# An attention and expert-routing kernel: a new order of work inside each pair of heads

## The chip, the cores and the metric

The kernel runs on one core of one Trainium2 chip. The metric is the device time of one execution in microseconds. In what follows PE is the matmul engine (TensorE), PEld its weight loads, DVE is VectorE, ACT is ScalarE, POOL is GpSimd and SP is SyncE, which only issues transfers here.

## The reference

The first half is attention with chunk selection for 4 batches, 8 heads, 768 positions and 64 channels. The second half sends every token to its best one of 8 experts.

```python
k_min, k_max = k_chunks.min(axis=3), k_chunks.max(axis=3)      # 24 chunks of 32 keys
ub = sum(maximum(q * k_min, q * k_max), over channels)          # a bound per query and chunk
top_chunks = the 6 chunks of largest ub, among those up to the query's own
scores = q @ k.T / 8, only in those chunks and only for keys up to the query
attn = softmax(scores);  x = attn @ v                           # heads side by side: (3072, 512)

logits = x @ w_gate;  expert = argmax(logits);  gate = softmax(logits)[expert]
out[token] = gate * (relu(x[token] @ w1[expert]) @ w2[expert])
```

## The kernel before

**Pairs.** The work is cut into 16 pairs of heads. Pair `i` is heads 2`hp` and 2`hp`+1 of batch `b`, with `b, hp = divmod(i, 4)`. Keys and queries lie transposed, channels on partitions: `KTE` and `QSB`, two buffers each, the pairs taking turns. The causal scores of a pair come in seven units `u`, each 128 keys by at most 384 queries for two heads (list `units`, L286). Units 0 and 1 belong to the first half of the queries (`qb` 0), units 2 to 6 to the second (`qb` 1).

**Steps of one pair.** Every step is a small function, and each belongs to one engine.

- `k_mm`, `q_mm` (PE, L192 and L219) transpose the loaded keys and queries into PSUM, half by half. `k_a` and `q_a` (ACT, L203, L228, L231) and `k_v`, `q_v` (DVE, L197, L198, L223) evict them. A cast on POOL (L229), put into the list `late`, fills the other half of `QSB`. `kse` (DVE) makes the chunk sums and differences.
- `ub` (PE, L238) computes the bounds, `ub_a` (ACT, L245) evicts them, `sel_mm` (PE, L250) transposes them. `sel_v` (DVE, L256 to L267) adds the causal bias, takes the eight largest of each row and marks the chunks that are not selected in `nsel`. `mask` (PE, L274) transposes the marks and `mask_a` (ACT, L280) copies them into rows of `QSB`, where they act as a penalty inside the score matmul.
- `scores` (PE, L298), `exps` (ACT, L314, then on POOL for blocks on the diagonal a triangle select, L318), `av` (PE, L331: probabilities times values, two heads on two halves of the array), `add` (DVE, L339: adds the unit's probabilities to those of the first unit, for the row sums). `o_ev(i, qb)` evicts the output of one half, on DVE (L346) or ACT (L344).
- `ud` (PE, L362 and L374, four 32-column tiles) computes row sums and unnormalized router logits, `ud_a` (ACT, L380) evicts them, `lgp_mm` (PE, L385) transposes them to `pl`. `lgp_v` (DVE, L391 and L395) takes the reciprocal and writes the scaled logits to `lgt`; a closure `sums` (POOL, L403 or L406), put into the list `sums_`, adds `lgt` to the batch's logits `lg`. `x_mm` (PE, L415) transposes the output to `px`, and `x_v` (DVE, L420) normalizes it into the token rows `xrow`.
- In pairs with `hp` 1 of batches 1 to 3 (`router`) the router of the batch before runs as well: `logits`, `expo`, `rank_mm`, `rank_v`, `gates`. `scatter` (POOL, L493) then writes the token rows to memory by expert.

**Order.** The order on every engine is written out by hand: `tc.manual_schedule` keeps each engine's instructions in program order. The main loop (L810) has four groups `g` for each pair `i`, and mixes steps of pair `i` with those of the pairs before and after: the output and router steps of pair `i`-1, the selection of pair `n` = `i`+1, the keys and queries of pair `m` = `i`+2. `flush(late)` and `flush(sums_)` emit the collected POOL steps at the place where they are called; `pieces` issues the next expert weight loads on POOL (L157). `first_pair` (L683) does pair 0 and the beginning of pair 1.

**Buffers.** The PSUM pool `ps_m` has three buffers; `pk`, `pq`, `pu`, `pt`, `pm`, `pl` and `px` take turns in them, in program order. `ps_s` has two buffers for scores and `ps_o` one for the output. In SBUF the probabilities have four buffers (`Pr`), and `lgt` has one.

**After the pairs.** `table` (DVE) works out which expert each tile of 128 tokens belongs to and where its rows are (`grow`). `gather` (POOL, L593) fetches the rows, `x_in` (SP, L605) transposes them, `up` (PE, L641) and `down` (PE, L653) are the expert's two matmuls, and the results are scattered to the output (POOL, L661).

The softmax here doesn't subtract the row's maximum and nothing guards it: scores larger than these inputs give would overflow.

## Time and profile before

| | us |
|---|---|
| median of 3 runs | 358.19 (357.07 to 358.97) |
| the profiled execution | 357.17 |
| its span, first to last instruction | 355.5 |
| PE busy in the span | 329.2 |
| ACT, DVE, POOL busy | 230.4, 229.5, 186.7 |
| first `ub` of pair 1 (end of most of the first pair) | 20.99 |
| first scores of unit 2 of pair 15 | 223.75 |
| first expert matmul | 236.43 |

The profile is one execution. A row of its timeline gives the start, the duration, the engine, the line, the operation, what is written and read, the number of instructions joined in the row, and in brackets how long the engine had been idle and what ended that. The duration of a row with several instructions runs from the start of the first to the end of the last. [...] the step from one start to the next says how much of PE's time an instruction takes. A busy share is a mean over the span, which here has two stages: the pairs of heads, in which all engines work, and the experts, in which DVE has little to do.

### The profile page before, as it was taken

To read this page: it belongs to the slowest core of one execution; us is meant where nothing else is said; L and a number is where in the kernel's file an instruction comes from. 1 tells how busy PE (TensorE), PEld (TensorE's weight loads), DVE (VectorE), ACT (ScalarE), POOL (GpSimd) and SP (SyncE) were. 2 spreads that over 40 slices of the span, in tenths; PEclk is the share of its full clock that TensorE was granted. 3 is DMA by queue.
4 is the path that set the end of the run, shared out by engine and by line. 5 is a ranking of instruction groups with operands and counts; after the bars stand their busy time and mean duration, and the time that the engine had idled before them with its cause. 6 is when DMAs were issued, how large, how long until landed. Compare 5 with 4: busy or idle time off the path is not lost. (4 is left out here: it accounts for less than half of the span.)

```text
span 355.5 us, 7585 instructions
## 1 busy us (share of the span) xinstructions
PE 329.2 (93%) x2382; PEld 177.2 (50%) x2392; DVE 229.5 (65%) x776; ACT 230.4 (65%) x373; POOL 186.7 (53%) x300
## 2 busy tenths in 40 slices
PE   7889999999999999999999999977995899999992
PEld 7545656556555555555565555534441344444440
DVE  6688999999999999999999999941730000000000
ACT  2588788788796887886887977613323454544551
POOL 8515434536475437284355477583574556655323
PEclk9999999999999999999999999989998999999999
DMA  9998998899585897765979954969694999998962
GB/s 175 205 209 152 167 184 169 153 190 167 104 211 113 161 178 155 152 171 114 186 137 181 182 122 113 209 124 197 137 227 121 227 185 216 194 231 160 216 154 80
DMA packets 132071, 59.83 MB, mean 168 GB/s; under 512 B 122811, under 2 KB 122813, under 8 KB 132032
## 3 DMA queue, kind: packets, MB, share of 16 engines
q1 hardware_dynamic: 120640, 29.91, 43.5%
q0 software_dynamic: 11392, 29.42, 40.0%
q8 instruction: 21, 0.34, 0.4%
q14 instruction: 18, 0.15, 0.1%
HBM read 56.14 MB, written 10.51 MB: 188 GB/s over the span
## 5 line engine op out<-in xcount | busy, mean ns | idle before, releaser
L339 DVE TENSOR_TENSOR Pa<-Pa,Pr 128x768 f32<-128x768 f32 (+2 forms) x109 | 80.5, 742 | 4.3
L318 POOL TENSOR_SCALAR_AFFINE_SELECT Pr<-Pr 128x256 f32<-128x256 f32 x78 | 36.9, 492 | 77.9 <-ACT Pr L314 77.9
L314 ACT ACTIVATE Pr<-ps 128x768 f32<-128x768 f32 x79 | 62.6, 819 | 10.7 <-ACT KTE L203 4.3
L653 PE MATMUL py<-w_all,hT 128*128 x220 | 52.4, 379 | 3.0 <-issue 1.7
L298 PE MATMUL ps<-QSB,KTE 128*128 128x384 bf16 (+4 forms) x352 | 50.4, 283 | 1.5 <-ACT Pr L314 0.2
L661 POOL DMA_INDIRECT out_dram<-y,ti_all x28 | 28.0, 1001 | 37.2 <-ACT y L660 32.1
L298 PEld LDWEIGHTS <-KTE 128*128 128x128 bf16 (+1 forms) x352 | 26.5, 102 | 28.4 <-issue 22.0
L641 PE MATMUL ph<-w_all,KTE 128*128 x116 | 31.1, 413 | 6.3 <-ACT h__3986 L644 3.6
L653 PEld LDWEIGHTS <-hT 128*128 128x128 bf16 x224 | 21.8, 98 | 29.5 <-issue 1.8
L314 ACT ACTIVATE Pa<-ps 128x768 f32<-128x768 f32 x32 | 26.0, 812 | 14.0 <-PE ps L298 12.6
L660 ACT ACTIVATE y<-py,gt_all 128x512 f32<-128x512 f32 x27 | 18.6, 687 | 25.0 <-PE py L653 19.4
L203 ACT ACTIVATE KTE<-pk 64x384 bf16<-64x384 f32 x60 | 29.3, 488 | 7.1 <-DVE kmn L198 6.7
L493 POOL DMA_INDIRECT xs_dram<-xrow,sli x24 | 25.6, 1065 | 7.8 <-issue 5.7
L641 PE MATMUL ph<-w_all,QSB 128*128 x94 | 22.6, 379 | 1.6 <-DMA QSB<-xgqT 1.5
L641 PEld LDWEIGHTS <-KTE 128*128 128x128 bf16 x120 | 12.3, 104 | 23.0 <-issue 9.6
L280 ACT ACTIVATE QSB<-pm 24x640 bf16<-24x640 bf16 x30 | 20.8, 692 | 2.8 <-PE pm L274 2.1
L614 DVE TENSOR_TENSOR ti_all<-xgqA,inv_i 128x1 int32<-128x1 int32 x9 | 1.4, 160 | 30.7 <-DMA xgqA<-xs_dram,grow 26.1
L157 POOL DMA_DIRECT2D w_all<-in_moe_w_dram x32 | 21.1, 663 | 0.0
L197 DVE TENSOR_REDUCE kmx<-pk 128x12 f32<-128x384 f32 x32 | 17.6, 549 | 3.2 <-PE pk L192 3.0
L593 POOL DMA_INDIRECT xgqT<-xs_dram,grow x14 | 14.8, 1058 | 9.1 <-issue 6.2
L593 POOL DMA_INDIRECT xgqA<-xs_dram,grow x14 | 14.4, 1029 | 8.6 <-issue 4.7
L614 DVE TENSOR_TENSOR ti_all<-xgqT,inv_i 128x1 int32<-128x1 int32 x8 | 1.3, 159 | 25.7 <-DMA xgqT<-xs_dram,grow 20.9
(318 smaller groups left out, 635.9 us busy)
## 6 DMA issues: line engine op xcount, KB each, us to landing
w_all<-in_moe_w_dram POOLq DMA_DIRECT2D x32, 512.0 KB
out_dram<-y,ti_all POOLq DMA_INDIRECT x28
t__115<-in_k_dram SPq DMA_DIRECT2D x2, 192.0 KB
t__118<-in_q_dram SPq DMA_DIRECT2D x2, 192.0 KB
t__121<-in_v_dram SPq DMA_DIRECT2D x2, 192.0 KB
t__218<-in_k_dram SPq DMA_DIRECT2D x2, 192.0 KB
t__240<-in_q_dram SPq DMA_DIRECT2D x2, 192.0 KB
t__243<-in_v_dram SPq DMA_DIRECT2D x2, 192.0 KB
```

The costliest lines, as they stand in the source:

```text
L157: nc.gpsimd.dma_start(out=dst, in_=src.rearrange("(c p) f -> p c f" if n < 2 else "(p c) f -> p c f", p=128))
L203: nc.scalar.activation(kte[0:64, hd, ts(hf, 384)], pt[64 * hd:64 * hd + 64, :], AF.Copy, bias=0.0, scale=0.125)
L280: nc.scalar.activation(qsb[64:64 + NCH, hd, 128:S], s["pm"][32 * hd:32 * hd + NCH, 128:S], AF.Copy)
L298: nc.tensor.matmul(ps[ds(h * n, n), hd, ds(c0, w)], lhsT=kte[:, hd, ds(kb * 128 + h * n, n)], rhs=qsb[:, hd, ds(qb * 384 + 384 - w, w)], s ...
L314: nc.scalar.activation(P[:], ps[:, :, 0:384], AF.Exp)
L318: nc.gpsimd.affine_select(out=pd, in_=pd, pattern=[[0, 2], [1, 128]], compare_op=ALU.is_ge, fill=0.0, base=0, channel_multiplier=-1)
L339: nc.vector.tensor_tensor(acc[:, :, 384 - w:384], acc[:, :, 384 - w:384], P[:, :, ds(c0, w)], ALU.add)
L493: d = nc.gpsimd.indirect_dma_start(out=xs_dram[:], out_offset=bass.IndirectOffsetOnAxis(ap=sli[:, u:u + 1], axis=0), in_=bst[b][f"xrow{u % ...
L593: d = nc.gpsimd.indirect_dma_start(out=xg_bufs[j % XB].bitcast(I32), out_offset=None, in_=xs_dram[:], in_offset=bass.IndirectOffsetOnAxis( ...
L641: nc.tensor.matmul(ph[:, fh, :], lhsT=xT[:, c, :], rhs=w_all[:, ds(wo + (c * F + fh * 512), 512)], start=(c == 0), stop=(c == NDC - 1), sk ...
L653: nc.tensor.matmul(py[:], lhsT=hT[:, c, :], rhs=w_all[:, ds(wo + (W1W + c * DM), DM)], start=(c == 0), stop=(c == NFC - 1))
L661: d = nc.gpsimd.indirect_dma_start(out=out[:], out_offset=bass.IndirectOffsetOnAxis(ap=fs[j]["ti"], axis=0), in_=y[:], in_offset=None, bou ...
```

## The change

The loop over four groups is written out as one sequence with a new order. Output 0 is evicted on ACT in all pairs. `ub` of pair `m` stands at the end of iteration `i`, behind `av` 4, 5 and 6; before, the same `ub` stood in the next iteration, behind `av` 0 and 1. `sel_mm` and `sel_v` follow scores 2 and 3, `mask` follows `k_mm(0)`, `ud` comes ahead of `av` 2 and 3, and `mask_a` comes ahead of exp 6 on ACT. `lgp_mm` and `x_mm(0)` follow scores 6. `q_a` copies the absolute values of both halves first and then the two halves of the queries. The chunk adds of units 1 and 4, 5 and 6 move to other places on DVE. The first pair computes the bounds with positions on partitions at once (`pt0`), without eviction and transposition, for five blocks of 128 positions, two and then three at a time.

```diff
@@ consts_first: the first pair's own bias and marks
-        nc.gpsimd.memset(cbias[:], 0.0)
...
+        cb0 = work.tile([128, NQ, NCH], FP32, tag="xrow", bufs=3, name="cb0")
...
+        ns0 = work.tile([128, NQ, 2, 32], BF16, tag="xrow", bufs=3, name="ns0")
...
+    def consts_bias():
+        nc.gpsimd.memset(cbias[:], 0.0)
...
@@ first_pair
         consts_last()
-        consts_route(colf)
-        prep[0]["ub"]()
-        prep[0]["ub_a"]()
+        pt = ps_m.tile([128, NQ, 2, NCH], FP32, tag="m", name="pt0")
+        for j in range(NQ):
+            for w_, nm in ((0, "qT"), (1, "qA")):
+                nc.tensor.matmul(pt[:, j], lhsT=s[nm][:].rearrange("p a c -> p (a c)")[:, ds(128 * j + 128, 128)],
+                                 rhs=KSD[0][:, w_, :, 0:NCH], start=(nm == "qT"), stop=(nm == "qA"),
+                                 skip_group_check=True)
         kt(1)
-        spin(8)
-        prep[0]["sel_mm"]()
-        spin(20)
+        spin(28)
...
         for _ in range(2):
             load_w(next(wnext))
+        consts_bias()
...
-        select(0)
-        mask_mm(0)
-        mask_in(0)
+        halves = (range(0, 2), range(2, NQ))
+        select(halves[0])
+        consts_route(colf)
+        mask_mm(halves[0])
+        mask_in(halves[0])
...
@@ the main loop, iteration i, as it is now
+            if i > 0:
+                if i < NP - 1 and not (hp == 2 and b > 0):
+                    pieces(i, 2 if router else 1)
+                if router:
+                    logits()
+                for u in (2, 3):
+                    scores(i, u)
+                    exps(i, u)
+                run(rout, i - 2, "x_mm", 1)
+                run(prep, n, "sel_mm")
+                add(i - 1, 6)
+
+                xv_first = hp != 2 or b == 0
+                if xv_first:
+                    run(rout, i - 2, "x_v", 1)
+                run(prep, n, "sel_v")
+                if not xv_first:
+                    run(rout, i - 2, "x_v", 1)
+
+                av(i, 0)
+                av(i, 1)
+                o_ev(i, 0, True)
...
+            for u in (4, 5):
+                scores(i, u)
+                if u == 5:
...
+                        if router:
+                            rank_mm()
+                            expo()
+                            rank_v()
+                            gates()
+                        run(prep, m, "k_mm", 0)
+                        run(prep, m, "k_a", 0)
+                        run(prep, n, "mask")
+                exps(i, u)
+
+            run(rout, i - 1, "ud")
+            run(rout, i - 1, "ud_a")
+            if i > 0:
+                add(i, 1)
+                run(prep, n, "mask_a")
+                run(prep, m, "k_v", 0)
+            av(i, 2)
+            av(i, 3)
+            add(i, 3)
+            flush(late)
+            if i < NP - 1:
+                pieces(i, 4)
+            scores(i, 6, True)
+            exps(i, 6)
...
+            if not router:
+                add(i, 4)
+            if i == NP - 2:
+                next(early_table)
...
+            run(rout, i - 1, "lgp_mm")
+            run(rout, i - 1, "x_mm", 0)
...
+            flush(sums_)
...
+            run(rout, i - 1, "lgp_v")
+            run(rout, i - 1, "x_v", 0)
+            run(prep, m, "k_mm", 1)
+            run(prep, m, "k_a", 1)
+            if n < NP:
+                for u in (0, 1):
+                    scores(n, u)
+                    exps(n, u)
+            run(prep, m, "k_v", 1)
+            for hf in range(2):
+                run(prep, m, "q_mm", hf)
+                run(prep, m, "q_v", hf)
+                run(prep, m, "q_a", hf, 0)
+            for hf in range(2):
+                run(prep, m, "q_a", hf, 1)
...
+            run(prep, m, "kse")
+
+            av(i, 4)
+            av(i, 5)
+            av(i, 6)
+            if router:
+                add(i, 4)
+            if i < NP - 1:
+                add(i, 5)
+            o_ev(i, 1, i >= NP - 2)
+            run(prep, m, "ub")
+            run(prep, m, "ub_a")
+            if hp == 0 and b > 0:
+                flush(sums_)
```

The removed lines of the loop, which held the same steps in the four groups, stand in the listing above.

## The prediction, written before the changed kernel had run

> **What bounds the kernel now.** I read the busy table first, then windows cut from one `ub` to the next (one pair of heads each), then the timeline of such a window, then the waits. "us" from the span's start.

> ```profile
> PE 329.2 (93%) x2382; PEld 177.2 (50%) x2392; DVE 229.5 (65%) x776; ACT 230.4 (65%) x373; POOL 186.7 (53%) x300
> ```
> ```profile
> 60.90:74.41 13.51, 13.44 (x116) 7.66 (x114) 12.62 (x38) 11.20 (x20) 6.42 (x12) 1.00 0.88 167
> 87.91:102.29 14.38, 14.08 (x129) 8.05 (x127) 13.83 (x50) 11.71 (x22) 7.55 (x13) 1.00 0.67 140
> 102.29:116.60 14.31, 13.57 (x116) 7.64 (x114) 13.61 (x39) 11.32 (x20) 7.20 (x13) 1.00 0.72 154
> ```
> The windows' columns are length, then busy PE, PEld, DVE, ACT, POOL. A plain pair takes 13.51 us with PE busy throughout, and DVE, 12.62 us, has only 0.9 us to spare. In the router pair (second row) and the one behind it DVE is the fuller engine. So PE sets the pace, and any wait on DVE reaches it at once. The end of a plain pair shows how near it comes:

> ```profile
> 65.14 0.50 PE L298 MATMUL ps<-QSB,KTE 128*64 128x256 bf16 x8
> 65.72 0.81 ACT L314 ACTIVATE Pr<-ps 128x768 f32<-128x768 f32 x1 [0.54 <-ACT KTE L203]
> 66.61 1.48 POOL L318 TENSOR_SCALAR_AFFINE_SELECT Pr<-Pr 128x256 f32<-128x256 f32 x2 [0.38 <-ACT Pr L314]
> 66.88 2.02 DVE L339 TENSOR_TENSOR Pa<-Pa,Pr 128x768 f32<-128x768 f32 x2
> 68.06 1.55 POOL L406 TENSOR_TENSOR lg<-lg,lgt 128x96 f32<-128x96 f32 x2
> ...
> 69.64 0.42 DVE L395 TENSOR_TENSOR lgt<-pl,rec 128x96 f32<-128x96 f32 x2 [0.41 <-POOL lg L406]
> 69.98 0.55 DVE L420 TENSOR_TENSOR xrow<-px,rec 128x384 bf16<-128x384 f32 x1
> ...
> 70.17 0.97 PE L219 MATMUL pq<-ident_f,t__966 128*128 128x128 f32 x6
> ```
> This is one chain: scores of unit 6, their exponential, two triangle selects on POOL, POOL's two sums (`sums`, which read the one `lgt` buffer), then DVE may overwrite `lgt`, which frees `pl`, whose PSUM buffer `q_mm(0)` needs (three buffers; `pl`, `px`, `pk`, then `pq`); `x_v(0)` frees `px` for `q_mm(1)`. Today PE has 70.17-65.14 = 5.03 us of other work between the ends of that chain, and the chain just fits:

> ```profile
> DVE lgt L395 <- POOL lg L406: 2.4, 6, 0.4
> ```
> Total, number, longest: six waits of 0.4 us in the stage from 33 to 223 us; covered, nothing more.

> [...] The rows above stand in program order, and a 0.41 us wait of `lgt` delays `xrow` behind it. [...] 102.83 to 103.47 from the last four `ub` matmuls to full-array scores is 0.64 us for 0.54 us of streaming, about 0.10 us a change. [...] a POOL sum takes 0.39 us alone and up to 1.09 us beside the chunk adds L339.

> **The change, part by part.**

> *Tiling modes: nothing.* In PE's order before and after I count three full-array groups, three two-tile groups and the excursion to four tiles for `ud`: eight changes a pair both times. 0.

> *Output 0 to ScalarE.* DVE loses one 0.55 us copy (L346) in pairs that are no router pairs; there it was on ScalarE already. ACT gains 0.50 us (row L344). With DVE at 12.1 it is no bound in a plain pair. But `ot` now waits on ACT for `av(0)`, `av(1)`, and exp 4, `k_a(0)`, exp 5, `ud_a`, `mask_a` and exp 6 queue behind it.

> *The new order of a plain pair,* with each step's length from start to start in today's trace. Zero is the start of `av(i-1,4)`. PE: av 4,5,6 1.99, `ub` 1.18, scores 2,3 0.72, `x_mm(1)` 0.39, `sel_mm` 0.43, av 0,1 1.45, scores 4,5 0.72, `k_mm(0)` 0.42, mask 0.38 (starts 7.30), `ud` 1.11, av 2,3 1.34, scores 6 0.43 (starts 10.13), `lgp_mm` 0.39, `x_mm(0)` 0.33, `k_mm(1)` 0.33, scores 0,1 0.66, `q_mm` 0.78 (starts 12.27): 13.05 us if nothing waits, 0.46 under today's. What goes is today's wait of scores 5 for exp 3 (0.24) and of `q_mm(1)` for `x_v` (0.15). The mask's selection fits barely: `sel_v` 4.95 to 7.06 (2.11 long), mask at 7.30.

> *The wait it adds.* Between scores 6 and `q_mm(0)` only `lgp_mm`, `x_mm`, `k_mm`, scores 0,1 are left: 2.14 us of PE cover where there were 5.03. On ACT, `ot` runs at 6.28 (last av row + 0.87), exp 4, two `k_a`, exp 5 take 0.70, 1.0, 0.70 and exp 5 starts at 8.45; `ud_a` 9.15, the two mask copies 9.52 to 10.92, exp 6 to 11.73. POOL: two selects of 0.39 from 11.81, two sums of 0.39 to 13.45. DVE: `lgt` 13.5 to 13.9, `x_v(0)` to 14.39. PE: `q_mm(0)` 13.95, `q_mm(1)` 14.43, pair over at **14.92**. Even with exp 6 at the first possible moment (scores 6 + 0.58) it is 14.65.
> POOL may be later still: the select of unit 5 can start at 9.34, in the middle of DVE's `add` 3 and 4 (about 9.1 to 11.1). If each of its reads waits for one add (0.9), the casts (0.94) and one weight issue (0.57) end at 12.8, not 11.2, and the pair takes 15.9. I take the middle, 15.4.

> *Sum over the pairs.* Six plain iterations (3, 4, 7, 8, 11, 12): 15.4-13.5 = +1.9 each, +11.4. Iteration 2 has one sum (L403, 0.40) in place of two: +1.6. Iterations 6 and 10 likewise, 15.1 against 14.3 and 14.5: +1.4. Router iterations 5, 9, 13 have no sums ahead of `lgt`; DVE's order there (logits 1.45, selection, ranks and gates 1.8 us ahead of `k_v(0)`, which frees `pk` for `pl`) gives 14.9 against 14.38: +1.5. Iteration 1 has no sums: -0.5. Together **+15.4**.

> *First pair.* `pt0` takes ten matmuls in place of `ub`, its 0.44 us eviction and three transposes. No row has this form; 0.109 us (an f32 transpose) to 0.140 (its weight load) each gives 1.1 to 1.4. With 28 spins of 0.055 the first mask transposes come at 12.45 in place of 13.45; `consts_route` (1.1 us DVE) moves behind the first selection, and `cbias` (three selects and a memset, 0.9 us POOL) behind the weight issues where POOL idled 3.8 us. **-1.0** (0 to -1.5).

> *End of the pairs.* PE waited 2.03 us for gathered rows at 236.43; the gather at 227.28 waited for DVE's `grow`, 3.5 us after scores 2 of pair 15 (223.75). In the new order `grow` ends about 1.0 after them, so the gather's 9.15 us fit PE's own work: **-2.0**, bounded by that wait (0 to -2.0). Iteration 14 has no `q_mm`: -0.2. Loads on SP keep their order and move with the pairs; w_all issues on POOL too (counted above); nothing waits for them.

> Sum: 15.4-1.0-2.0-0.2 = **+12.2**. The profiled execution took 357.17 us, 355.5 of it span: 369.4. The median of the runs, 358.19, stands 1.0 above it, so I forecast **370.4 us**.

> **Rivals.**
> [...] Every POOL read meets an add: 15.9 in all plain pairs, +2.4 times six, iterations 2, 6, 10 another 0.6 each, routers unchanged: +20.2, less 3.2: 375. For it: L318 rows of 1.48 us for two. Against: at 11.8 DVE stands still, waiting for that very sum. 0.17.
> *Lighter.* exp 6 early and POOL free: 14.65, +1.15 times six, the other terms halved (+1.75): +8.6, less 3.2: 364. 0.14.
> *Faster.* The sums are done before DVE comes to `lgt`; then a plain pair takes 13.1 and the DVE-bound ones 0.6 less: -0.4 times eight, -0.6 times five, less 3.2: -9.4, 349. It decides if POOL's sums end before 11.7, that is 1.75 us sooner than worked out. For it: DVE loses 0.55 us, two PE waits vanish. Against: scores 6 are issued at 10.13. 0.08.
> *Nothing.* The wait shrinks to about 0.4 a pair and the first pair and the end pay for it, or the grouping does no more than keep eight mode changes: 358. 0.04.

> **How the numbers follow.** The main case has 0.57, and 370.4 is its time. Three cases are slower, 0.88; one within 0.5% (some 1.8 us, about what a measurement here tells from no change), 0.04; one faster, 0.08. The range, 360.0 to 377.0, takes in the light and the heavy case with some 2 us beyond them for the first pair and the router pairs, and leaves the other two out.

> **What would show it.** DVE `lgt` waiting for POOL's `lg` some 2 us in nine or ten iterations, with PE idle or stalled ahead of `pq`; plain pairs near 15 us; exp 6 behind the mask copies on ACT; the gather at most 1.5 us after scores 2 of pair 15. A plain pair under 13.6 us, or no wait ahead of `lgt`, proves me wrong; waits of mask for `nsel` instead would mean the selection, not the sums, is the cost.

## The result, and the profile after

The changed kernel takes **382.18 us** (median of 4 runs, 380.25 to 384.68) where the kernel before takes 358.38 on the same chip. The ratio is **1.067, with a 95% interval of 1.060 to 1.074**. The forecast was 370.4 us with a range of 360 to 377. The direction was right, and in the pairs the mechanism too; the loss that was forecast, 12.2 us, is half of what came, and the measured time lies outside the range. Ratios and their intervals leave out executions that took over 1.5% more than the fastest of the same kernel, so a ratio can be smaller than the quotient of two medians, and three of the traces below (`ud` late in every pair, the first try of the matmuls, the old first pair) are of such executions.

Line numbers of the changed kernel are 9 higher up to its main loop: scores L307, exponentials L323, selects L327, `av` L340, `add` L348, `lgt` L404, `q_mm` L228, the sums L412 and L415. The busy table and the clock row of the page after come first. PE has 4.3 us more busy time, but its share has fallen from 93% to 88%, and the row of the granted clock now has dips in the middle, where the kernel before has none.

```profile
PE 333.5 (88%) x2390; PEld 184.9 (49%) x2400; DVE 231.7 (61%) x764; ACT 235.0 (62%) x382; POOL 186.7 (49%) x303
...
PEclk9998999999999989999989999989899999999999
```

The clock row of the kernel before:

```profile
PEclk9999999999999999999999999989998999999999
```

To place the loss I cut both traces at the same step, the first scores of unit 2 of each pair. In parentheses is what half clock takes from a stage at most: half the length of its stretches, in which the granted clock was 0.50.

| stage, us | before | after | difference |
|---|---|---|---|
| start to scores 2 of pair 1 | 31.27 (0) | 36.32 (1.7) | +5.05 |
| pairs 1 to 13 | 180.10 (0) | 196.57 (3.4) | +16.47 |
| pair 14 | 12.37 (0) | 12.09 (0) | -0.28 |
| scores 2 of pair 15 to the first expert matmul | 12.68 (0) | 14.48 (1.7) | +1.80 |
| to the first `down` | 12.25 (1.7) | 14.55 (1.7) | +2.30 |
| to the end | 106.77 (2.6) | 106.34 (0.9) | -0.43 |

The `ub` of the next pair now stands ahead of these scores, 1.18 us of PE's time. It counts in the first row and is missing in that of pair 14. Half clock takes up to 5.1 us more than before over all rows.

The chain that carried the forecast is in the timeline of the changed kernel, in iteration 7. Columns are start, duration, engine, line, operation, and in brackets the idle time before and its releaser.

```profile
130.26 1.39 ACT L289 ACTIVATE QSB<-pm 24x640 bf16<-24x640 bf16 x2
130.29 1.67 POOL L238 CAST QSB<-qT 64x384 bf16<-64x384 f32 x2
130.32 2.46 DVE L348 TENSOR_TENSOR Pa<-Pa,Pr 128x768 f32<-128x768 f32 x2 [0.24 <-PE po L340]
...
130.75 0.50 PE L307 MATMUL ps<-QSB,KTE 128*64 128x256 bf16 x8
...
131.68 0.82 ACT L323 ACTIVATE Pr<-ps 128x768 f32<-128x768 f32 x1
...
132.66 0.77 POOL L327 TENSOR_SCALAR_AFFINE_SELECT Pr<-Pr 128x256 f32<-128x256 f32 x2
...
133.40 0.85 POOL L415 TENSOR_TENSOR lg<-lg,lgt 128x96 f32<-128x96 f32 x2
...
134.28 0.42 DVE L404 TENSOR_TENSOR lgt<-pl,rec 128x96 f32<-128x96 f32 x2 [1.35 <-POOL lg L415]
...
134.80 0.97 PE L228 MATMUL pq<-ident_f,t__1821 128*128 128x128 f32 x6 [1.75 <-issue]
```

With zero at the start of `av` 4 of pair 6, 120.73, as in the forecast, scores 6 start at 10.02 (forecast 10.13), exp 6 at 10.95 behind the mask copies (forecast 10.92), `q_mm(0)` at 14.07 (forecast 13.95). The same waits over the stage from 33 to 241 us, as total, number, longest:

```profile
PE pq L228 <- issue: 15.6, 9, 2.3
...
DVE lgt L404 <- POOL lg L415: 9.1, 6, 2.4
DVE lgt L404 <- POOL lg L412: 4.2, 3, 2.1
```

Nine waits of `lgt`, where six of 0.4 us stood, and nine stalls of PE ahead of `q_mm`, 15.6 us in all; the pairs are 13.1 us longer apart from the clock. "Issue" hides the cause in PE's row; the DVE rows name it.

What the forecast did not have is in the windows (length, then busy PE, PEld, DVE, ACT, POOL, the granted clock, DMA share, GB/s): first a plain pair, then the 3.41 us that hold the stall above, then the 3.41 us behind it.

```profile
73.29:88.24 14.95, 13.21 (x113) 7.93 (x112) 12.65 (x36) 11.63 (x21) 5.88 (x13) 1.00 0.79 150
...
132.82:136.23 3.41, 1.66 (x14) 1.01 (x13) 2.06 (x7) 2.08 (x4) 2.98 (x8) 1.00 0.90 132
136.23:139.64 3.41, 3.41 (x20) 1.66 (x15) 2.38 (x7) 1.82 (x4) 0.21 (x1) 0.50 1.24 243
```

The plain pair takes 14.95 us for 13.21 of PE work. In the second row PE is busy for half of the time, and in the third its granted clock is 0.50: `av` 4, 5 and 6 take 3.40 us where they took 1.99. That pair took 16.65 us, and the same happened once more, at 197.67 us (a pair of 17.20).

The end and the start, in the timeline:

```profile
239.73 2.20 DVE L348 TENSOR_TENSOR Pa<-Pa,Pr 128x768 f32<-128x768 f32 x2 [1.00 <-PE po L340]
...
243.20 1.66 DVE L534 CAST nt<-nt_i 128x8 f32<-128x8 int32 x1
...
248.19 0.17 DVE L571 SCALAR_TENSOR_TENSOR grow<-ej,loc 128x11 int32<-128x11 f32 x1
...
249.16 1.09 POOL L602 DMA_INDIRECT xgqT<-xs_dram,grow  x1 [3.27 <-issue]
...
251.67 0.52 PE L371 MATMUL pu<-Pa,dcol 128*32 128x384 f32 x3 [1.75 <-DVE Pa L348]
...
268.78 2.62 PE L650 MATMUL ph<-w_all,KTE 128*128 x7 [3.30 <-DMA KTE<-xgqA]
```

The same steps of the table and the gather in the kernel before, where scores 2 of pair 15 start at 223.75:

```profile
221.73 0.43 DVE L525 CAST nt<-nt_i 128x8 f32<-128x8 int32 x1
...
226.31 0.17 DVE L562 SCALAR_TENSOR_TENSOR grow<-ej,loc 128x11 int32<-128x11 f32 x1
...
227.28 1.09 POOL L593 DMA_INDIRECT xgqT<-xs_dram,grow  x1 [2.21 <-issue]
```

`grow` ends 3.4 us after scores 2 of pair 15 (244.98), where it ended 2.7 us after them before and about 1.0 was forecast. So the gather starts 4.18 us after them, not 3.5 as before and not at most 1.5 as forecast. The `ud` of pair 14, now ahead of `av` 2 and 3, waits twice for DVE steps that stand behind the table (0.75 us for `lgt`, 1.75 for the adds), half clock follows from 252.29, and later gathered rows (`xgqA`) are waited for 3.30 us.

```profile
9.48 0.39 PE L742 MATMUL pt<-KSD,qT 128*128 128x48 f32 x2 [1.20 <-DVE qT L724]
9.71 0.39 PE L742 MATMUL pt<-KSD,qA 128*128 128x48 f32 x2
...
27.27 0.52 PE L201 MATMUL pk<-ident_f,t__406 128*128 128x128 f32 x3 [1.90 <-DMA t__406<-in_k_dram]
...
29.57 0.34 PE L307 MATMUL ps<-QSB,KTE 128*128 128x384 bf16 x1 [0.86 <-ACT QSB L289]
```

Each row of `pt0` is one f32 product. The profile shows it as two records (x2), each 0.28 us long and 0.112 us apart from start to start; from product to product it is 0.223 us, and ten take 2.24 us. The first `ub` of pair 1 starts at 20.88, 0.11 us earlier than before. Then the keys of pair 2 are waited for, and after that the scores of pair 1 wait for the mask copies. The kernel before waits half as long for these keys, and not at all for the copies:

```profile
26.43 0.52 PE L192 MATMUL pk<-ident_f,t__402 128*128 128x128 f32 x3 [0.96 <-DMA t__402<-in_k_dram]
```

### The profile page after: what moved, and what is told of

The parts are those of the page before. It is cut to its first block, busy times and chain, and to the rows that moved or that the text cites. A ratio compares the mean times of both kernels' runs of the same rounds, so it can differ in the third digit from the quotient of the medians.

```text
span 380.3 us, 7596 instructions
## 1 busy us (share of the span) xinstructions
PE 333.5 (88%) x2390; PEld 184.9 (49%) x2400; DVE 231.7 (61%) x764; ACT 235.0 (62%) x382; POOL 186.7 (49%) x303
## 5 line engine op out<-in xcount | busy, mean ns | idle before, releaser
L348 DVE TENSOR_TENSOR Pa<-Pa,Pr 128x768 f32<-128x768 f32 (+2 forms) x109 | 86.0, 789 | 7.4 <-PE po L340 4.2
L327 POOL TENSOR_SCALAR_AFFINE_SELECT Pr<-Pr 128x256 f32<-128x256 f32 x78 | 32.0, 431 | 111.9 <-ACT Pr L323 111.4
L323 ACT ACTIVATE Pr<-ps 128x768 f32<-128x768 f32 x79 | 63.7, 809 | 3.8 <-DVE Pa L348 2.8
L307 PE MATMUL ps<-QSB,KTE 128*128 128x384 bf16 (+4 forms) x352 | 49.2, 284 | 1.9 <-ACT QSB L289 1.2
L307 PEld LDWEIGHTS <-KTE 128*128 128x128 bf16 (+1 forms) x352 | 26.6, 103 | 27.4 <-issue 19.7
L650 PE MATMUL ph<-w_all,KTE 128*128 x116 | 28.7, 388 | 7.1 <-issue 3.7
L502 POOL DMA_INDIRECT xs_dram<-xrow,sli x24 | 27.2, 1134 | 6.5 <-issue 6.2
L323 ACT ACTIVATE Pa<-ps 128x768 f32<-128x768 f32 x32 | 25.9, 810 | 1.1 <-PE ps L307 0.7
L238 POOL CAST QSB<-qT 64x384 bf16<-64x384 f32 x30 | 24.2, 834 | 0.0
L237 ACT ACTIVATE qA<-pq 128x384 f32<-128x384 f32 x30 | 14.2, 490 | 15.2 <-DVE qT L232 15.1
L602 POOL DMA_INDIRECT xgqT<-xs_dram,grow x14 | 15.0, 1072 | 11.8 <-issue 7.8
```

The source lines that it names most:

```text
L238: late.append(lambda: nc.gpsimd.tensor_copy(out=qsb[0:64, 0, ts(hf, 384)], in_=s["qT"][0:64, hf]))
L307: nc.tensor.matmul(ps[ds(h * n, n), hd, ds(c0, w)], lhsT=kte[:, hd, ds(kb * 128 + h * n, n)], rhs=qsb[:, hd, ds(qb * 384 + 384 - w, w)], s ...
L323: nc.scalar.activation(P[:], ps[:, :, 0:384], AF.Exp)
L327: nc.gpsimd.affine_select(out=pd, in_=pd, pattern=[[0, 2], [1, 128]], compare_op=ALU.is_ge, fill=0.0, base=0, channel_multiplier=-1)
L348: nc.vector.tensor_tensor(acc[:, :, 384 - w:384], acc[:, :, 384 - w:384], P[:, :, ds(c0, w)], ALU.add)
L502: d = nc.gpsimd.indirect_dma_start(out=xs_dram[:], out_offset=bass.IndirectOffsetOnAxis(ap=sli[:, u:u + 1], axis=0), in_=bst[b][f"xrow{u % ...
```

## The experiments

Theory: the sums behind the late selects hold `lgt`, `lgt` holds `pl`, and `pl` holds `q_mm`. Rivals: the queues of ACT and DVE are late anyway; POOL's reads beside DVE's adds are the cost, wherever they stand. The chips differ: the kernel before took 352.2 us on one of them and 357.7 to 358.4 on the others. So each kernel is compared by its ratio to the kernel before on the same chip, with the 95% interval; the changed kernel's is 1.067. That a ratio is the same on every chip is not tested. Traces are of one execution each.

**A second logits buffer.**

```diff
-            lgt = work.tile([128, 6, 2, 2, E], FP32, tag="lgt")
+            lgt = work.tile([128, 6, 2, 2, E], FP32, tag="ge" if i % 2 else "lgt")
...
-        cj = work.tile([128, n], FP32, tag="t_cj")
+        cj = work.tile([128, n], FP32, tag="sh")
...
-        inv = work.tile([128, n], FP32, tag="t_inv")
+        inv = work.tile([128, n], FP32, tag="cand")
```

The second buffer is that of `ge`, a tile of the expert table, and two small tiles of the table move to other buffers.

> The changed kernel (382.2 us) with a second buffer for the scaled logits, so that DVE no longer waits for POOL's sums of the pair before; the order on every engine is as in the changed kernel. Theory 'sums behind the late selects': the 2 us waits of lgt go in all pairs, PE's stall ahead of q_mm goes with them, a plain pair comes to about 13.5 us (13.05 of PE work and today's excess of 0.46), and the stretches at half clock from 136 to 140 and 198 to 201 us vanish because no long stall is left: 364 to 369 us. Rival 'the queues are late anyway' (exp 6 behind the mask copies, DVE fuller): the wait only moves to the next step, 1 us or less is saved per pair, 374 to 380 us.

Measured: 365.27 us, ratio 1.019 (1.014 to 1.024). Timeline, at the same step of iteration 3:

```profile
74.40 0.42 DVE L404 TENSOR_TENSOR lgt<-pl,rec 128x96 f32<-128x96 f32 x2
...
74.82 0.85 POOL L415 TENSOR_TENSOR lg<-lg,lgt 128x96 f32<-128x96 f32 x2
74.92 0.96 PE L228 MATMUL pq<-ident_f,t__966 128*128 128x128 f32 x6 [0.44 <-PE ps L307]
```

The sums are as late as they were, but `lgt` no longer waits for them, and PE's stall is 0.44 us. Pairs 1 to 13 take 181.87 us with no half clock, 14.7 less than in the changed kernel, and a plain pair 13.66 (13.51 before; 13.05 was my sum of PE's steps). One buffer decides between theory and rival: the order on all engines is unchanged. What is left of the loss is mostly at the start of its trace: scores 2 of pair 1 come at 38.30 us, 7.0 later than before, with 3.4 us of half clock and the moved `ub` (1.18) in that, and the keys of pair 2 at 28.88.

**Sums earlier, one buffer.** `flush(sums_)` is added behind `o_ev(i, 0, True)`.

> The changed kernel with only POOL's sums moved: they stand behind the eviction of output 0, ahead of the selects of units 5 and 6, with one logits buffer. Theory 'sums behind the late selects': the same effect as a second buffer, 364 to 371 us, at most 2 us from it. If a second buffer helps and this does not, POOL's reads beside DVE's adds[...] are the cost and not the place in the queue: 372 to 380 us.

Measured: 369.73 us, ratio 1.034 (1.029 to 1.038); pairs 184.88 us. The place in POOL's queue is the cost: no wait of `lgt` for the sums is left in its trace between 33 and 241 us. It lies 4.5 us from the second buffer, where at most 2 were expected; 3.0 of them are in the pairs.

**`ud` late in every pair.** `ud` and `ud_a` move behind `exps(i, 6)`.

> The changed kernel with ud and ud_a behind the scores and exponential of unit 6 in every pair, as in the kernel before; the sums and the single logits buffer stay as changed. Theory 'sums behind the late selects': scores 6 come 1.1 us earlier, exp 6 no longer stands behind ud_a, and ud adds 1.1 us to the 2.14 us of PE cover ahead of q_mm, so the 2 us wait of lgt shrinks to 0.5 us or less and the pairs come near the two-buffer case: 365 to 372 us. Rival 'it is POOL's access beside the adds, not the place of exp 6': the wait stays above 1.5 us, 377 to 383 us.

Measured: 380.71 us, ratio 1.076 (1.070 to 1.082), no better than the changed kernel. From its waits, stage from 44 to 241 us:

```profile
PEld pl L394 <- ACT ud L389: 20.8, 12, 1.8
```

My expectation overlooked that the mask copies stay ahead of exp 6 and that `ud_a` now stands behind it: PE waits for `ud_a` instead, twelve times, and the waits of `lgt` for the sums remain (9.3 us in six). So exp 6 starts 1.86 us after scores 6, where the changed kernel has 0.94 and the kernel before 0.59: the edit made it later against its scores, not earlier. The steps of the new order depend on one another, and one of them taken back makes a new wait. The time lies in the rival's range, but does not speak for the rival, since the earlier sums had settled it.

**Less cover alone, in the kernel before.**

```diff
-                    av(i, 4)
-                    av(i, 5)
                     if not router:
...
+                    av(i, 4)
+                    av(i, 5)
                     av(i, 6)
```

> The kernel before with one thing changed: av 4 and 5 stand behind q_mm, beside av 6, as in the changed kernel; scores 6, ud, mask copies and sums keep their places. PE's cover between scores 6 and q_mm falls from 5.03 us to about 3.65, and the chain from scores 6 to the freed pl takes 4.9. Theory 'cover': about 1.25 us of stall ahead of q_mm in the nine pairs with sums, less in the two where DVE is the bound, so pairs 8 to 11 us longer: ratio 1.02 to 1.035. Rival 'without a late exp 6 there is no wait': ratio 0.995 to 1.01.

Measured: ratio 1.037 (1.032 to 1.042), a little above the expected size; pairs 190.43 us, 10.3 more than before. But the waits are others than I expected. Its timeline:

```profile
70.39 2.20 DVE L339 TENSOR_TENSOR Pa<-Pa,Pr 128x768 f32<-128x768 f32 x2
...
70.69 2.15 POOL L406 TENSOR_TENSOR lg<-lg,lgt 128x96 f32<-128x96 f32 x2
...
72.87 0.42 DVE L395 TENSOR_TENSOR lgt<-pl,rec 128x96 f32<-128x96 f32 x2
...
73.39 0.97 PE L219 MATMUL pq<-ident_f,t__962 128*128 128x128 f32 x6 [0.22 <-PE pk L192]
```

Sums and adds run side by side, slow each other, and end together, so DVE shows no wait: further on in the same timeline, at 84.70 us, one add takes 1.14 us and the sum beside it 1.08, where in the kernel before an add with no POOL instruction beside it takes 0.95 and a sum with no add beside it 0.39. PE's loss is spread: scores for mask copies 3.8 us in ten waits, `lgp_mm` for `ud_a` 2.4 in eleven, `q_mm` 2.5 in nine, `x_mm` 2.6 in three. So `av` 4 and 5 covered more than the one chain that I named, and that the size came out near the forecast is in part luck. Exp 6 is not late here (0.59 us after scores 6, as before), and still the pairs lose 10.3 us, where the whole change costs them 13.1 apart from the clock. Lost cover alone can account for most of the loss; what the later exp 6 adds, no run isolates.

**Output 0 on ACT alone, in the kernel before.** `dve_ot = False`.

> The kernel before with output 0 on ACT in all pairs and nothing else. On record I costed it at nothing: DVE is 0.55 us emptier in a plain pair and ACT 0.50 us fuller, PE sets the pace: ratio 0.995 to 1.005. Rival: output 0 on ACT delays exp 4 and with it the whole chain to lgt, 0.2 to 0.5 us in nine pairs: ratio 1.005 to 1.013.

Measured: ratio 1.003 (0.999 to 1.007), which can't tell it from nothing. One trace shows more: most plain pairs take 13.86 us where they took 13.51, and in the one from 70 us on `lgt` waits 0.78 us for the sums instead of 0.41; the pairs behind router pairs are 0.5 and 0.3 shorter. All thirteen come to +1.5 us. In this version `ub_a` still stands ahead of the eviction on ACT, which it does not in the changed kernel, so the price need not carry over.

**A second logits buffer in the kernel before.**

> The kernel before with a second logits buffer. If its six waits of lgt for POOL's sums (2.4 us in all) are covered, as I read them, nothing changes: 357.2 to 358.2 us. If each reaches PE, 2.4 us go: 355.3 us.

Measured: 350.91 us beside 352.21, ratio **0.995 (0.993 to 0.998)**. The pairs are 1.7 us shorter. The six with a wait of 0.4 us, which I read as covered, are 0.1 to 0.2 us shorter each, 0.95 of the 2.4 us in all; the two behind router pairs (6 and 10), which showed no such wait, give as much again, and the router pairs are 0.07 longer each. This version is the fastest of all, by half a per cent.

**Matmuls in the stall, first try.** 24 matmuls on constants ahead of `q_mm`.

> The changed kernel with 24 matmuls on constants (0.055 us each, 1.3 us) ahead of the first q_mm of the next keys in iterations 2 to 13, where PE waits 1.8 to 2.3 us; their result is not used. Theory 'a long PE wait halves the clock afterwards': the wait of lgt stays, the period of a plain pair stays at 14.9, but no stretch at half clock is left in the pairs, the mean clock of the runs comes to 0.98 or more from 0.964 to 0.975, and two stretches of 1.7 us each are saved: 377.5 to 380.5 us. Rival 'the clock has nothing to do with the waits': stretches stay, 382 to 385 us.

Measured: 396.46 us, ratio 1.116 (1.110 to 1.122). They write to the scores buffer of unit 1, and standing behind its exponential they waited for it:

```profile
76.13 2.32 PE L937 MATMUL ps<-ones_b 128*128 128x128 bf16 x24 [1.94 <-ACT Pr L323]
```

The stall was not filled: the matmuls waited as long as it had lasted (1.94 us) and then took their own time, and most plain pairs are 1.4 us longer than in the changed kernel (16.34 us). Nothing follows for the clock.

**The same matmuls in place.**

```diff
                 for u in (0, 1):
                     scores(n, u)
+                    if u == 1 and 1 < i < NP - 2:
+                        for _ in range(24):
+                            nc.tensor.matmul(st[n]["ps1"][:, 1, 384:512], lhsT=ones_b[:], rhs=ones_b[:], start=True,
+                                             stop=True, skip_group_check=True)
                     exps(n, u)
```

> The changed kernel with 24 matmuls on constants (1.3 us) between the scores of unit 1 of the next pair and its exponential, in iterations 2 to 13; their result is not used, and this time they wait for no exponential. PE's idle ahead of q_mm falls from about 1.8 us to 0.5 while the wait of lgt stays. Theory 'a 3.41 us window with half its PE time idle halves the clock of the next one': no half-clock stretch between 46 and 240 us, plain pairs at 14.9 to 15.1 us, mean clock 0.98 or more: ratio 1.05 to 1.06. Rival 'the clock follows something else': stretches stay there, ratio 1.065 to 1.08.

Measured: 381.23 us, ratio 1.067 (1.061 to 1.073). The window from `lgp_mm` of iteration 7 to that of iteration 8, here first and in the changed kernel second:

```profile
132.10:147.06 14.96, 14.54 (x140) 9.27 (x136) 12.65 (x37) 11.73 (x21) 6.05 (x13) 1.00 0.82 150
```

```profile
131.18:147.83 16.65, 14.90 (x117) 8.64 (x113) 12.75 (x37) 11.62 (x21) 6.06 (x13) 0.90 0.74 135
```

With PE kept busy in the wait, the wait of `lgt` stays (9.1 us in six, as in the changed kernel) and the half clock goes: no stretch between 46 and 240 us, mean clocks of the runs 0.980 to 0.985 where the changed kernel has 0.964 to 0.975. The total missed my expectation, because the three router pairs have no stall and pay 1.7 to 2.4 us each for the filling.

**The end of the pairs.** The `ud` of pair 14 goes behind `exps(15, 6)`.

```diff
+            if i < NP - 1:
+                run(rout, i - 1, "ud")
+                run(rout, i - 1, "ud_a")
...
                 pieces(i, 4)
+                run(rout, i - 1, "ud")
+                run(rout, i - 1, "ud_a")
```

> The changed kernel with one step of the last pair where it was before: the row sums and router logits of pair 14 come behind the scores and exponential of unit 6 of pair 15, not ahead of av 2 and 3. Theory 'the last pair's sums wait for DVE behind the table': PE's waits for Pa (0.75 and 1.75 us) find cover, and the stretch at half clock from 252 to 256 us goes: 377.5 to 380 us. Rival 'DVE is late there whatever PE does' (exponentials wait for the adds as well): under 1 us, 381 to 382.5 us.

Measured: 382.23 us median, but from 376.19 to 386.53. Two of the four runs lie below all of the changed kernel's and two do not, so the time decides nothing. In the trace, from scores 2 of pair 14 to the first `down` it takes 36.94 us, 1.7 of it half clock, which leaves 35.2. The changed kernel has 41.12 with 3.4, which leaves 37.7; two more traces with the same order at the end (the old first pair, the matmuls in place) leave 37.3 and 36.5. So the `ud` is worth some 1.2 to 2.5 us, in single traces.

**The old first pair, and the new first pair alone.** First the changed main loop behind the old first pair:

> The changed main loop with the first pair of the kernel before. Theory 'iteration 0 lost it' (mask copies ahead of the scores of pair 1 with nothing to cover them): the first pair gives 0.2 us either way, so 381 to 383 us, with the first logits transposes again near 43.3 us. Rival 'the new first pair lost it' (weights issued earlier, the keys of pair 2 land 0.8 us later, a stretch at half clock from 30 to 34 us): those transposes come 1.5 to 2.5 us earlier and the time is 379.5 to 381 us. My forecast of 1.0 us gained by the first pair would give 383.2.

Measured: ratio 1.065 (1.057 to 1.074), no difference that can be told from 1.067. In its trace scores 2 of pair 1 come at 35.50 us, 0.8 earlier, with as much half clock as in the changed kernel. Then the old main loop behind the new first pair:

> The kernel before with the new first pair alone. On record I gave this part 1.0 us of gain. The trace of the changed kernel shows ten pt0 matmuls of 0.223 us each, 2.24 us, where I had 1.1 to 1.4, and first scores only 0.16 us earlier; so now: 0.1 to 0.3 us of gain, 357.4 to 358.2 us beside 357.7. If the weight transfers issued earlier hold up the keys of pair 2 (27.3 us in place of 26.4), a loss of 0.5 to 1 us instead: 358.2 to 358.8.

Measured: 353.24 us beside 352.21, ratio 1.003 (0.9995 to 1.006). A gain of 1.0 us is excluded; a small loss is likely, not certain.

**Repairs together.** The second buffer, pair 0's `av` 4 and 5 behind the mask copies, the `ud` of pair 14 late, and the table ahead of the adds:

```diff
+            if i == NP - 2:
+                for _ in early_table:
+                    pass
             if i > 0:
                 add(i, 1)
```

> The changed kernel with four repairs: a second logits buffer; av 4 and 5 of pair 0 back behind the mask copies; the expert table on DVE ahead of the adds of pair 14; the row sums of pair 14 behind the scores of unit 6 of pair 15. If the pairs (lgt), iteration 0 and the end of the pairs are the whole loss, the time comes to within 1% of the kernel before (ratio 0.99 to 1.01). If the new order has another cost of its own (fuller ACT, the keys of pair 2 later), ratio 1.015 to 1.03, as with the second buffer alone (1.019).

Measured: ratio 1.023 (1.016 to 1.031), no better than the second buffer alone. Then without moving the table:

> The changed kernel with three repairs: a second logits buffer, av 4 and 5 of pair 0 back behind the mask copies, the row sums of pair 14 behind the scores of unit 6 of pair 15; the table on DVE stays where the change has it. Theory 'ud ahead of av 2 and 3 lost the end of the pairs': from the logits of pair 14 to those of pair 15 it takes 11.5 to 12 us (15.7 in the changed kernel, 10.7 before) and the ratio is 1.003 to 1.015. Rival 'DVE behind the table lost it whatever PE does': 13.5 us or more for that step, ratio 1.015 to 1.025.

Measured: ratio 1.025 (1.019 to 1.030). From one logits transposition to the next it takes 11.79 us, as the theory said, and the ratio is the rival's. The timelines of the two show where it went, first with the table moved, then without:

```profile
232.95 0.80 PE L307 MATMUL ps<-QSB,KTE 128*128 128x256 bf16 x4 [3.32 <-ACT Pr L323]
```

```profile
245.82 6.39 PE L650 MATMUL ph<-w_all,KTE 128*128 x16 [5.18 <-DVE gt_all L625]
```

With the table first, the adds are late, the exponentials find no free buffer, and PE waits 3.32 us. Without it PE waits 5.18 us ahead of the first expert matmul, where the profile names a DVE copy out of the gathered rows (`gt_all`); from the first gather to that matmul it takes 13.1 us, 9.15 in the kernel before. In both half clock follows. At the start, too, the repair moved the wait instead of ending it. Behind the mask copies `av` 4 and 5 cover them, but no longer the chunk sums that the early `ub` of pair 2 needs, here with the table moved:

```profile
37.63 0.76 PE L247 MATMUL pu<-qT,KSD 128*64 128x320 f32 x4 [1.74 <-DVE KSD L219]
```

And with the old first pair in addition:

> The same three repairs with the first pair of the kernel before. If the new first pair gives the 1.0 us that I forecast, this is 1.0 us slower than the three repairs; if it gives 0.2 us, nothing can be told (ratio within 0.004 of them); if it costs (keys of pair 2 later), this is 1 to 2 us faster, ratio 1.000 to 1.010.

Measured: ratio 1.018 (1.012 to 1.024), and the intervals overlap. In the two traces the keys of pair 2 arrive at 26.46 us with the old and 27.97 with the new first pair, and scores 2 of pair 1 come 1.5 us apart.

## Why the forecast was right and wrong

In the two traces the change costs 24.9 us where 12.2 were forecast. With the moved `ub` counted where it was, the end of the pairs holds 7.2 us of the missing 12.7, the start 4.9 and the pairs 1.1; the experts take 0.4 off. Up to 5.1 us of it are half clock.

**Bound and mechanism in the pairs: right.** PE sets the pace, and with only 2.14 us of its work left between scores 6 and `q_mm` the chain through exp 6, selects, sums, `lgt` and `pl` stalls it. The trace follows the worked-out times within 0.15 us, and the second buffer takes 14.7 of the 16.5 us in the pairs away. The weight lies on the lost cover: exp 6 starts only 0.35 us later against its scores than before, and in the run with less cover alone, which has no such delay, the pairs still lost 10.3 us.

**The plain pair: too long by choice.** I worked out 14.92 us and took 15.4, a middle between that and the case in which each POOL read waits for one add (0.9 us), which was an assumption of mine. Measured: 14.94 to 14.98 in iterations 3, 4, 8 and 12, and, without the clock's part, 14.95 in 7 and 15.5 in 11. Casts and adds did slow each other (1.67 us for two casts in the row shown, 0.95 in a plain pair of the kernel before; 2.46 for the two adds, where one with no POOL instruction beside it takes 0.95), but that part of POOL's queue had room: the casts end at 131.96, before exp 6 does (132.50). The six plain iterations gave +9.2 in place of +11.4; 6 and 10 gave +2.4 in place of +1.4, iteration 2 +1.1 (+1.6), the router ones +0.6 (+1.5), iteration 1 -0.2 (-0.5). Without the clock's part the pairs are +13.1 in place of +15.4. One reading behind the router term was wrong: in the window of the router pair PE is busy for 14.08 us and DVE for 13.83, so DVE is the fuller engine only in the pair behind it (13.61 against 13.57).

**A clock at full speed: the step that was missing.** I priced a stall at its own length. In these traces every half-clock stretch but the one at the end lasts 3.41 us or a multiple of it, and in each trace they begin on one grid of 3.41 us: in the changed kernel at 30.42, 136.23, 197.67, 252.29 and 269.35 us, 31, 18, 16 and 5 such steps apart. There a gap of 1.75 us, which left PE busy for 49% of one such window, was followed by half clock; other windows as empty were not (48% from 211.33 us in the same trace, and see the last section). In all, up to 5.1 us more went to half clock than in the kernel before. For the 3.4 us in the pairs the matmuls in place show that PE's idle time is the cause; for the rest it is read from the traces.

**End of the pairs, -2.0 and -0.2: the step that failed most.** "`grow` ends about 1.0 after them" was wrong: it ended 3.4 us after scores 2, later than before (2.7), so the gather came no sooner, and PE still waits for rows (3.30 us, 2.03 before). The first add there waits for `av` 2, which now stands behind `ud`, and one conversion in the table took 1.66 us where it had taken 0.43. I also costed nothing for the `ud` of pair 14, which the new order puts ahead of `av` 2 and 3 in pair 15, in front of DVE's late adds; that is the moved step whose queue I did not follow. The three stages of the end came to +3.8 us, 1.7 of it clock, although a `ub` of 1.18 had left them, in place of -2.2; undoing that `ud` alone brought some 1.2 to 2.5 us back in a trace. Why the same edit brought nothing beside a second buffer (PE then waited 5.18 us ahead of the first expert matmul) stays open.

**First pair, -1.0: wrong.** The ten `pt0` matmuls took 2.24 us, not 1.1 to 1.4: 0.112 us a record was inside the estimate, but each product is two records. Up to the first `ub` of pair 1 the gain is 0.11 us. And the new order of iteration 0 was put at nothing. The start is 5.05 us longer, of which 1.18 is the moved `ub` and up to 1.7 half clock. About 2.2 us remain: the mask copies stand ahead of the scores of pair 1 with no `av` between, and the keys of pair 2 come late. The copies are not the whole of it, since with `av` 4 and 5 back behind them `ub` of pair 2 waited 1.68 to 1.74 us for DVE's chunk sums in three traces, and apart from the clock the start was no shorter. With `pt0` these keys came at 25.9 to 29.4 us in ten traces, without it at 26.4 to 27.0 in six, though they were asked for at nearly the same time; why is open.

**Output 0 on ACT, 0: within the noise of the times.** In one trace most plain pairs are 0.35 us longer, so the waits of `lgt` had no room there. The second buffer in the kernel before shows it from the other side: "covered, nothing more" was not quite so.

## What to carry to other kernels

Before work is moved from between two ends of a chain, count what it covers, and look for the one buffer that lets a slow neighbour into the chain: a second one was worth some 17 us in the new order and 1 to 2 in the old. Price a stall of the bounding matmul engine not at its length alone: here up to 1.7 us more followed, at a granted clock of 0.50, where stalls left about half of a 3.41 us window empty. And follow a reordered loop through its first and last iterations separately, because there the steps that cover each other are missing.
